# Blocks 8 to 15 of a float64 weight conversion placed in a hand-written order of steps, behind the first copies of y

## The chip, the cores and the metric

The kernel runs on one core of a Trainium2 chip. The metric is the device time of one execution in microseconds (us); lower is better. A core has five engines with an instruction stream each: PE (matmul; its weight loads are listed as PEld), DVE (vector), ACT (scalar), POOL and SP. SP, ACT and POOL also issue DMA transfers. Each engine takes its instructions in program order, and an instruction waits at the head of its stream until what it reads has been written and what it overwrites has been read.

## What is computed

Two blocks follow each other. The first filters every channel of `x` along the sequence in the frequency domain; the second is a small feed-forward network with the activation h * sigmoid(h).

```python
X = np.fft.rfft(x, axis=1)                     # x: (8, 3008, 256)
y = np.fft.irfft(X * (filt_r + 1j * filt_i)[None], n=3008, axis=1)
t = y.reshape(24064, 256)
h = t @ w_in                                   # (256, 2048)
g = h * (1.0 / (1.0 + np.exp(-h)))
return (g @ w_out).astype(np.float32)          # (2048, 256)
```

`w_in` and `w_out` reach the kernel as float64, two 32-bit words per value. The chip's engines work in float32 here, so the kernel converts them itself.

## The kernel before

**Tiles.** The 2048 hidden channels are 16 blocks of 128 (j = 0 to 15), in 8 pairs (jp = 0 to 7). The tokens of a batch are two halves of three token pairs each, 48 token pairs in all. One *step* is one token pair with one pair of blocks, so there are 384 steps, and the first eight (steps 0 to 7) are the first token pair with jp = 0 to 7. Both products use a scheme of seven multiplications in place of eight: a step has seven `hidden` matmuls (line 974), and one step later seven `project` matmuls (line 1041) that add up the output in PSUM. The scheme needs sums of weights (S1 to S4, `combine_weights`), sums of tokens (`tokens`, tile `ty`), and sums of the activated values `g` (all on DVE, line 945).

**A step** has eight rounds (0 to 7). `hidden` and `project` yield after each matmul, so that one matmul of each stands in a round. `hidden` copies the partial sums out of the bank `px` three times on ACT (lines 982, 989, 995, tile `abc`), adds them to the bank `pyz` on DVE (line 945: g0 in round 1, g2 in round 4, g1 in round 7) and applies the activation on ACT (line 978). `px` and `pyz` have one buffer each, so the next step's first matmul on `pyz` waits until DVE has read g1.

**Other work** is hung into this order by `put(step, round, piece)`: it is issued when that round is reached. Here belong the seven remaining pieces of batch 1's first transform, `stage1(u)` (line 413, tile `pa`: two matmuls of 512 columns; line 418: two copies on ACT; line 426: four stores on POOL, `store_rows`), at steps u - 1, round 3, for u = 2 to 7.

**Conversion of a weight block** (512 values in each of 128 partitions) splits each float64 into exponent and mantissa:

- `bits_of_weights`, DVE, lines 1173 and 1175: exponent bits `e` and mantissa bits `m` from the high word.
- `convert_weights`, ACT, lines 1180 and 1181: both to float. For blocks 0, 2 and 6 two more on ACT, lines 1186 and 1187.
- `round_weights`, DVE, line 1193: the low word added to the mantissa; line 1195 (other blocks): the exponent to the bits of a power of two; line 1199: the sign put on it.
- `place_weights`, DVE, line 1208: mantissa times power, two multiplications of 256 columns, into `w_t`, the weights for the matmuls.

Then `combine_weights(jp)` forms four sums of a pair of blocks, DVE, four additions of 256 columns (line 945).

**The stretch that the change touches** begins after batch 0's transforms. `stage3(g)` for g = 0 to 3 (line 715, tile `pd`) makes the first half of y; eight copies (line 729) bring it to SBUF, two of them on DVE (g = 2 and 3, h = 1), six on ACT. Before `stage3` there are idle matmuls (`idle_wide`, line 1279) that compute nothing. The order in the source is, shortened:

```python
placed(4, 5); rounded(6, 7); placed(6, 7)
rounded(8); placed(8)
gp.tensor_copy(out=gate, in_=w_t[:, 4, A11, 0, 0:1])
for u in range(2): second["store_rows"](u)
idle_wide(12)
for g in range(4): part["stage3"](g)
nc.sync.dma_start(out=wi_t, in_=wi_dram.ap())
second["load_x"](2); weights(10, 11, 12); second["load_x"](3); weights(13)
```

The copy to `gate` (POOL, line 1364) holds the stores of batch 1's first two pieces, which come behind it on POOL, until block 8 is placed. The load of `wi_t` (SP, line 1370) overwrites a table that `stage3` reads, and so holds the loads behind it on SP. Once the order of steps begins, blocks 9 to 15 are converted one per step: block j at step j - 9, its bits, float conversion and rounding in round 1, its placing in round 5.

Of the kernel before, what the change touches and what calls it, by code (L numbers as in the profile page):

```python
# [65 lines left out]
LAG = 1  # L66

A11, A12, S3, A22, S1, S2, S4 = range(7)
ROUNDS = 8


# [49 lines left out]
def laid_out(inputs):  # L121

    row = np.empty((128, 2 * NG), int)
    p = np.arange(128)
    for j in range(4):
        s0, tau = slot_residue(0, 0, j), (1 if j % 2 == 0 else -1)
        for half in range(2):
            off, t = (s0, tau) if half == 0 else (94 - s0, -tau)
            mine = p[(p // 32 == j) & (p % 2 == half)]
            row[mine] = off + t * np.arange(2 * NG) + 94 * np.arange(16)[:, None]  # L130
    filt = np.stack([inputs["filt_r"][row], inputs["filt_i"][row]], axis=1)
    w_in, w_out = inputs["moe_w_in"], inputs["moe_w_out"]
    w_in = w_in.reshape(128, 2, NJ, 128).transpose(2, 0, 1, 3).reshape(NJ, 128, 256)
    moe_w = np.concatenate([w_in, w_out.reshape(NJ, 128, 256)], axis=2)
    return dict(x=inputs["x"], x_first=first_quarters(inputs["x"][0]), filt_a=filt[:, :, 0:4], filt_b=filt[:, :, 4:], moe_w=moe_w)


# [124 lines left out]
def kernel(  # L262
# [64 lines left out]

    w_t = cpool.tile([128, NJP, 7, 2, 128], FP32)
    warm = cpool.tile([128, 1], FP32)
    bias_t = cpool.tile([128, 5], FP32)  # L330
    gate = cpool.tile([128, 1], FP32)
    x_all = xpool.tile([128, 2, 2, 2 * C], FP32)
# [23 lines left out]
    def spectral(b):  # L356
# [304 lines left out]
        def rows_first(g):  # L661

            if g in (2, 3):
                room = t4pool.tile([128, 4, C], FP32, name=f"q_{b}_{g}", tag="t4")
                tiles = room[:, 0:2], room[:, 2:4]
            else:
                tiles = [pool.tile([128, 2, C], FP32, name=f"q_{b}_{g}_{i}", tag=tag) for i, (pool, tag) in
                         enumerate(((zpool, "z"),) * 2 if g == NG - 1 else ((qpool, "q"), (opool, "o")))]
            for i, qt in enumerate(tiles):
                copy, queue = (nc.scalar.copy, nc.scalar) if i == 0 or g < 4 else (nc.vector.tensor_copy, nc.sync)  # L670
                copy(out=qt, in_=halves[g][i])
                a0 = 8 * g + 4 * i
                queue.dma_start(out=d2[a0:a0 + 4].rearrange("a n h c -> (a n) h c"), in_=qt)
# [119 lines left out]
    def put(step, rnd, piece, *args):  # L793

        pending.append((step + rnd / ROUNDS, len(pending), lambda: piece(*args)))

    last_part = [None]

    def plan(b, part):
# [2 lines left out]

        if b == 1:
            for u in range(2, 8):
                put(at + u - 49, 3, part["stage1"], u)
        else:
            put(at - {2: 80, 3: 120}.get(b, 128), 0, part["reverse_x"])
            early_fold = (-73, ((-68, 3), (-68, 5), (-67, 5), (-66, 5))), (-89, ((-82, 5), (-81, 3), (-81, 5), (-75, 5)))
# [211 lines left out]
    def project(step):  # L1020
# [16 lines left out]
        for c, k, i, h in order:  # L1037
            if i not in acc[pair]:
                acc[pair][i] = accps.tile([128, 2, 256], FP32, name=f"acc_{pair}_{i}", tag=f"a{i}")

            nc.tensor.matmul(out=acc[pair][i][:, h, 0:n], lhsT=w_t[:, jp, c, 1], rhs=g[:, k, 0:n],  # L1041
                             start=(jp == 0 and h == 0), stop=last, skip_group_check=True)
            if last and pair == len(pairs) - 1:
                drain_last(pair, i, h, n, acc[pair])
            elif last and (h == 1 or i == 3):
                drain(pair, i)
            yield
# [66 lines left out]

    PLACES = (((A11, 1), (A11, 2)), ((S3, 1), (A12, 2)))
    raws = {}

    def places(j, w):  # L1120
        first, by = PLACES[j % 2][w]
        return w_t[:, j // 2, first:first + by + 1:by, w]

    def columns(ap, w):

        if w == 0:
            return ap.rearrange("p (k n) -> p k n", k=2)
        return ap.rearrange("p (q k i) -> p k q i", q=4, k=2)

    def load_weights(j, queue=None):  # L1130

# [22 lines left out]
    def bits_of_weights(*js):  # L1154

        for j in js:
# [9 lines left out]
            else:  # L1166
# [2 lines left out]
            lo, hi = words[:, :, 0], words[:, :, 1]  # L1169
            ef, mf = e.bitcast(FP32), m.bitcast(FP32)  # L1170
            ends = (lo, hi) if j in (2, 3, 6, 7) else (m, e)
            raws[j] = lo, hi, e, m, ef, mf, ends[0].bitcast(FP32), ends[1].bitcast(FP32), ends[1]
            v.tensor_scalar(out=e, in0=hi, scalar1=20, scalar2=0x7ff,
                            op0=ALU.logical_shift_right, op1=ALU.bitwise_and)
            v.tensor_scalar(out=m, in0=hi, scalar1=0xfffff, scalar2=None, op0=ALU.bitwise_and)

    def convert_weights(*js):
        for j in js:
            _, _, e, m, ef, mf, *_ = raws[j]
            nc.scalar.activation(out=ef, in_=e, func=AFT.Relu, bias=bias_t[:, 0:1])  # L1180
            nc.scalar.activation(out=mf, in_=m, func=AFT.Identity, scale=2.0 ** -20, bias=1.0)
        for j in js:
            if j in (0, 2, 6):

                e, ef = raws[j][2], raws[j][4]
                nc.scalar.activation(out=ef, in_=ef, func=AFT.Relu, scale=-1.0, bias=bias_t[:, 1:2])
                nc.scalar.activation(out=e, in_=ef, func=AFT.Identity, scale=-float(1 << 23),
                                     bias=bias_t[:, 2:3])

    def round_weights(*js):  # L1190
        for j in js:
            lo, hi, e, m, ef, mf, mo, _, _ = raws[j]
            v.scalar_tensor_tensor(out=mo, in0=lo, scalar=2.0 ** -52, in1=mf, op0=ALU.mult, op1=ALU.add)
            if j not in (0, 2, 6):
                v.tensor_scalar(out=e, in0=ef, scalar1=255.0, scalar2=float(1 << 23),
                                op0=ALU.min, op1=ALU.mult)
        for j in js[::-1]:
            hi, e, eo = raws[j][1], raws[j][2], raws[j][8]
            v.scalar_tensor_tensor(out=eo, in0=hi, scalar=0x80000000, in1=e,
                                   op0=ALU.bitwise_and, op1=ALU.bitwise_or)  # L1200

    def place_weights(*js, eng=None):
        for j in js:
            mo, eo = raws.pop(j)[6:8]
            for w in range(2):
                cols = slice(256 * w, 256 * w + 256)
                dst = places(j, w) if w == 0 else places(j, w).rearrange("p k (q i) -> p k q i", q=4)
                (eng or v).tensor_tensor(out=dst, in0=columns(mo[:, cols], w), in1=columns(eo[:, cols], w),  # L1208
                                         op=ALU.mult)

    def load_exact(j):
        for k in range(2):
            nc.sync.dma_start(out=places(j, 0)[:, k], in_=moe_w[j][:, 128 * k:128 * k + 128])
            nc.sync.dma_start(out=places(j, 1)[:, k].rearrange("p (q i) -> p q i", q=4),
                              in_=columns(moe_w[j][:, 256:512], 1)[:, k])

    def combine_weights(jp, part=None, eng=None):

        eng = eng or v

        def w(c):
            return w_t[:, jp, c]
        if part != 1:
            combine(eng, w(S1), w(S3), w(A22), ALU.add)
            combine(eng, w(S2), w(S1), w(A11), ALU.subtract)
# [13 lines left out]
    def converted(*js):  # L1239
        if wide:  # L1240
            convert_weights(*js)

    def split(*js):
        bits(*js)
        converted(*js)

    def rounded(*js):
        if wide:
            round_weights(*js)

    def placed(*js, eng=None):
        if wide:
            place_weights(*js, eng=eng)
        else:
            for j in js:
                load_exact(j)
# [3 lines left out]
    wx3_t = qpool.tile([128, 2, C], FP32, name="wx3", tag="q").rearrange("p a c -> p (a c)")[:, 0:384].rearrange(  # L1260
        "p (k m) -> p k m", k=3)
    nc.scalar.dma_start(out=wx3_t, in_=wx3_dram.ap())
    for i, value in enumerate((-896.0, 255.0, 255.0 * (1 << 23))):
        nc.gpsimd.memset(bias_t[:, i:i + 1], value)
    for j in range(4):
        for i in range(2):
# [86 lines left out]
    weights(9)  # L1353
    for u in range(2):
        second["stage1"](u, False)
    converted(6, 7)
    converted(8)
    rounded(4, 5)
    placed(4, 5)
    rounded(6, 7)  # L1360
    placed(6, 7)
    rounded(8)
    placed(8)
    gp.tensor_copy(out=gate, in_=w_t[:, 4, A11, 0, 0:1])
    for u in range(2):
        second["store_rows"](u)
    idle_wide(12)
    for g in range(4):
        part["stage3"](g)
    nc.sync.dma_start(out=wi_t, in_=wi_dram.ap())  # L1370
    second["load_x"](2)
    weights(10, 11, 12)
    second["load_x"](3)
    weights(13)
    early[0] = None
    plan_rest(0, part)
    for g in (4, 5):
# [3 lines left out]
        put(step, 0, lambda t=t, dram=dram: nc.sync.dma_start(out=t, in_=dram.ap()))  # L1381
    for b in range(1, B):
        plan(b, second if b == 1 else spectral(b))
    for j in range(9, NJ):
        if j < 12:
            put(j - 9, 1, lambda j=j: (split(j), combine_weights(j - 8), rounded(j)))
        else:
            put(j - 9, 1, lambda j=j: (split(j), rounded(j)))
        put(j - 9, 5, placed, j)
        if j % 2:  # L1390

            put(*((j - 8, 5) if j < 15 else (j - 9, 6)), combine_weights, j // 2, 0)
            put(*{13: (j - 8, 7), 15: (j - 8, 1)}.get(j, (j - 7, 5)), combine_weights, j // 2, 1)

        if j < 11:
            put(j - 9, 1, weights, j + 5)

    per = len(PAIRS) * 2

# [76 lines left out]
```

## Time and profile before

| what | value |
|---|---|
| median of three runs | 2507.9 us (2505.73 to 2509.2) |
| the profiled execution's own time | 2507.82 us |
| span in its profile (first to last instruction) | 2506.0 us |
| PE busy | 2485.7 us (99%) |
| DVE busy | 1764.2 us (70%) |
| ACT busy | 1095.1 us (44%) |
| POOL busy | 430.8 us (17%) |
| first `hidden` matmul (step 0) | 63.93 us after the span's start |
| first `hidden` matmul of step 8 | 127.49 us |

The profile lists every instruction of one execution with its start and duration, and what ended the idle time ahead of it. A window table gives the busy time of each engine in a stretch, the granted TensorE clock (PEclk, 1.00 is full speed) and how busy the DMA engines were. The chain of waits follows the work back from the last instruction. Instructions of one engine overlap a little, so the distance from one start to the next (the *pitch*) is shorter than a duration. DMA queues are named q1 (SP), q10 (ACT), q0 (POOL) and q8 (PE's own instructions).

### The profile page before, as it was taken

The page shows a single profiled execution, that of the slowest core. Times are in us where ns is not written, and L with a number is a line of the kernel's source. Part 1 is how long each engine was busy: PE and PEld are TensorE (multiplying, and loading weights), DVE is VectorE, ACT ScalarE, POOL GpSimd, SP SyncE. Part 2 cuts the span into 40 slices and gives each one's busy share as a digit, 9 for nine tenths or more (in the row PEclk, how much of TensorE's full clock was granted, in tenths as well). Part 3 has the DMA queues.
Part 4 walks back from the last instruction along what each step waited for, and adds up shares of the span by engine and source line. Part 5 has one row for each costly group of instructions (what it writes and reads, how often), then busy time and mean ns, then how long its engine had stood idle before and what let it go on. Part 6 is the DMA issues. An engine that isn't in the chain of part 4 may idle for free.

```text
span 2506.0 us, 42228 instructions
## 1 busy us (share of the span) xinstructions
PE 2485.7 (99%) x16196; PEld 2128.4 (85%) x16196; DVE 1764.2 (70%) x3633; ACT 1095.1 (44%) x3011; POOL 430.8 (17%) x674
## 2 busy tenths in 40 slices
PE   8999999999999999999999999999999999999999
PEld 6688888888888888888888888888888888888988
DVE  8866677777767777777777867777677767655544
ACT  4444444444444444444444444444444444444443
POOL 2211212112121121211222112211121111101100
PEclk9999999999999999999999999999999999999999
DMA  8522232213232032420334203321142211200000
GB/s 304 156 67 95 73 85 64 76 51 80 61 89 77 26 88 52 115 65 15 89 67 104 58 26 82 87 68 43 27 110 58 55 43 34 64 21 9 17 9 17
DMA packets 139802, 170.68 MB, mean 68 GB/s; under 512 B 20860, under 2 KB 113372, under 8 KB 138716
## 3 DMA queue, kind: packets, MB, share of 16 engines
q1 hardware_dynamic: 115536, 120.77, 18.2%
q0 software_dynamic: 22080, 44.10, 6.8%
q8 instruction: 127, 2.08, 0.3%
q10 hardware_dynamic: 1984, 3.11, 0.3%
q14 instruction: 75, 0.61, 0.1%
HBM read 96.06 MB, written 81.26 MB: 71 GB/s over the span
## 4 chain that ended last, share of the span: by engine, by line
PE 96%; DVE 2%; ACT 1%; DMA 0%; issue 0%; POOL 0%; SPq 0%; DVEq 0%; ACTq 0%
PE acc L1041 45%; PE px L974 26%; PE pyz L974 19%; PE pd L751 1%; PE pf L483 1%; PE pc L579 1%; PE pb L541 1%; DVE g L945 1%; PE pc L657 0%; PE pa L389 0%; PE pb L523 0%; DMA w_t<-in_x_first_dram 0%; DVE w_t L1208 0%; DVE w_t L945 0%; PE pc L637 0%
## 5 line engine op out<-in xcount | busy, mean ns | idle before, releaser
L1041 PE MATMUL acc<-g,w_t 128*128 128x256 f32 (+1 forms) x5376 | 1507.8, 376 | 3.0 <-ACT o L764 2.5
L1041 PEld LDWEIGHTS acc<-g,w_t 128*128 128x128 f32 x5376 | 1016.4, 190 | 154.1 <-ACT o L764 15.3
L945 DVE TENSOR_TENSOR g<-pyz,abc 128x256 f32<-128x256 f32 (+1 forms) x1152 | 479.7, 416 | 476.9 <-ACT abc L995 236.5
L945 DVE TENSOR_TENSOR g<-g 128x256 f32<-128x256 f32 (+3 forms) x1152 | 590.6, 513 | 196.7 <-ACT g L978 183.6
L974 PE MATMUL px<-ty,w_t 128*128 128x256 f32 (+1 forms) x2304 | 677.9, 376 | 1.1 <-ACT abc L989 0.6
L978 ACT ACTIVATE g<-g 128x256 f32<-128x256 f32 (+1 forms) x1152 | 472.9, 411 | 238.1 <-DVE g L945 238.1
L945 POOL TENSOR_TENSOR s<-s 128x256 f32<-128x256 f32 (+1 forms) x329 | 252.4, 785 | 1418.9 <-DVE s L1059 1093.4
L974 PEld LDWEIGHTS px<-ty,w_t 128*128 128x128 f32 x2304 | 434.2, 190 | 59.9 <-ACT abc L989 3.9
L974 PE MATMUL pyz<-y,w_t 128*128 128x256 f32 (+1 forms) x1536 | 452.4, 376 | 1.2 <-DVE g L945 1.1
L974 PEld LDWEIGHTS pyz<-y,w_t 128*128 128x128 f32 x1536 | 283.5, 189 | 46.0 <-DVE g L945 5.8
L989 ACT COPY abc<-px 128x256 f32<-128x256 f32 (+1 forms) x384 | 141.3, 368 | 368.1 <-PE px L974 368.1
L978 ACT ACTIVATE g<-px 128x256 f32<-128x256 f32 (+1 forms) x384 | 145.8, 380 | 303.3 <-PE px L974 303.3
L995 ACT COPY abc<-px 128x256 f32<-128x256 f32 (+1 forms) x384 | 141.5, 368 | 308.5 <-PE px L974 308.4
L974 PE MATMUL px<-y,w_t 128*128 128x256 f32 (+1 forms) x768 | 227.9, 378 | 2.5 <-DVE y L729 2.5
L974 PE MATMUL pyz<-ty,w_t 128*128 128x256 f32 (+1 forms) x768 | 226.0, 376 | 0.2 <-DVE g L945 0.2
L974 PEld LDWEIGHTS px<-y,w_t 128*128 128x128 f32 x768 | 144.1, 190 | 24.3 <-issue 2.6
L974 PEld LDWEIGHTS pyz<-ty,w_t 128*128 128x128 f32 x768 | 142.2, 190 | 21.5 <-DVE g L945 1.0
L982 ACT COPY abc<-px 128x256 f32<-128x256 f32 (+1 forms) x384 | 135.1, 352 | 37.0 <-PE px L974 37.0
L503 POOL DMA_DIRECT2D d<-tf x96 | 48.5, 506 | 216.0 <-DVE tf L433 210.6
L1059 ACT COPY s<-acc 128x512 f32<-128x512 f32 (+1 forms) x94 | 54.2, 577 | 47.6 <-issue 28.5
L600 POOL DMA_DIRECT2D d<-low x36 | 22.3, 618 | 286.3 <-DVE low L596 286.3
L473 DVE TENSOR_TENSOR uf<-x_all 120x512 f32<-120x512 f32 (+1 forms) x72 | 60.2, 864 | 0.3 <-issue 0.3
(141 smaller groups left out, 1356.8 us busy)
## 6 DMA issues: line engine op xcount, KB each, us to landing
t<-d SPq DMA_DIRECT2D x84, 256.0 KB
t<-d SPq DMA_DIRECT2D x224, 96.0 KB
out_dram<-s SPq DMA_DIRECT2D x64, 256.0 KB
d<-q POOLq DMA_DIRECT2D x48, 256.0 KB, 5.3
x_all<-in_x_dram SPq DMA_DIRECT2D x96, 96.0 KB
x_all<-xr SPq DMA_DIRECT2D x96, 96.0 KB
d<-tf POOLq DMA_DIRECT2D x96, 96.0 KB, 2.7
d<-tq POOLq DMA_DIRECT2D x96, 96.0 KB, 2.8
```

The lines of the kernel that those rows point to most:

```text
L473: nc.vector.tensor_tensor(out=out, in0=in0, in1=in1, op=op)
L483: nc.tensor.matmul(out=ps[q][32 * k:32 * k + 32], lhsT=wq_t[rows, k], rhs=rhs[k][rows], start=True, stop=True)
L503: nc.gpsimd.dma_start(out=d1[par, :, grp, at:at + 4], in_=part[rows].rearrange("p q n c -> p (q n) c"))
L541: nc.tensor.matmul(out=ps[k, ri][32 * j:32 * j + 32, a, :], lhsT=dn_t[rows, 4 * (g + a) + at, :], rhs=t2s[g + a][rows, at, :], start=True, ...
L945: eng.tensor_tensor(out=out, in0=in0, in1=in1, op=op)
L974: nc.tensor.matmul(out=out, lhsT=w_t[:, jp, c, 0], rhs=rhs, start=start, stop=True, skip_group_check=True)
L978: nc.scalar.activation(out=g[:, k, 0:n], in_=g[:, k, 0:n] if src is None else src, func=AFT.Silu)
L982: nc.scalar.copy(out=sums[:, 0, 0:n], in_=xo)
L989: nc.scalar.copy(out=sums[:, 1, 0:n], in_=xo)
L995: nc.scalar.copy(out=sums[:, 2, 0:n], in_=xo)
L1041: nc.tensor.matmul(out=acc[pair][i][:, h, 0:n], lhsT=w_t[:, jp, c, 1], rhs=g[:, k, 0:n], start=(jp == 0 and h == 0), stop=last, skip_group ...
L1059: copy(out=s[:, 2 * i:2 * i + 2, 0:n], in_=acc[pair][i][:, :, 0:n])
```

## The change

- **Layout.** `laid_out` on the host reorders the weights, so that `place_weights` is a single operation of 512 contiguous columns per block. In `w_t` the output halves of A12 and S3 change places (`OUT_PLACE`).
- **Integer mantissas.** The mantissa stays an integer with its leading one put in by line 1175's second operation; the factor 2^-20 goes into the placing. ACT no longer converts mantissas. Both exponent operations are on ACT for every block, and line 1195 is gone.
- **Order.** Behind the placing of block 7 come the copies of y on DVE and the token sums at once. Block 8 (its bits and exponent are still done ahead), and blocks 9 to 15, are spread over steps 0 to 6 in a written list, in smaller pieces.
- **One copy moves** from DVE to ACT (`rows_first`, g = 4, second half).
- **Loads.** `load_x(2)`, block 10, `load_x(3)`, blocks 11 and 12 are issued directly behind block 9's load, ahead of the load of `wi_t`. Block 13 follows at step 1, 14 and 15 at step 2.
- **Batch 1's pieces** u = 2 to 7 stand one step earlier, at steps u - 2.
- **Gate and idle matmuls.** `gate` reads block 7's weights. 15 idle matmuls instead of 12 ahead of `stage3`, and 2 new ones behind it.

```diff
-                put(at + u - 49, 3, part["stage1"], u)
+                put(at + u - 50, 3, part["stage1"], u)
...
-            v.tensor_scalar(out=m, in0=hi, scalar1=0xfffff, scalar2=None, op0=ALU.bitwise_and)
+            v.tensor_scalar(out=m, in0=hi, scalar1=0xfffff, scalar2=0x100000, op0=ALU.bitwise_and,
+                            op1=ALU.bitwise_or)
     def convert_weights(*js):
         for j in js:
...
+            nc.scalar.activation(out=ef, in_=e, func=AFT.Relu, scale=-1.0, bias=bias_t[:, 0:1])
+            nc.scalar.activation(out=e, in_=ef, func=AFT.Relu, scale=-float(1 << 23), bias=bias_t[:, 1:2])
+    def add_weights(*js):
+        for j in js:
+            lo, m, mo = raws[j][0], raws[j][3], raws[j][5]
+            v.scalar_tensor_tensor(out=mo, in0=lo, scalar=2.0 ** -32, in1=m, op0=ALU.mult, op1=ALU.add)
...
+            v.scalar_tensor_tensor(out=places(j), in0=mo, scalar=2.0 ** -20, in1=eo, op0=ALU.mult, op1=ALU.mult)
...
+    second["load_x"](2)
+    weights(10)
+    second["load_x"](3)
+    weights(11, 12)
     converted(6, 7)
     converted(8)
     rounded(4, 5)
     placed(4, 5)
     rounded(6, 7)
     placed(6, 7)
-    rounded(8)
-    placed(8)
-    gp.tensor_copy(out=gate, in_=w_t[:, 4, A11, 0, 0:1])
+    gp.tensor_copy(out=gate, in_=w_t[:, 3, S3, 0, 0:1])
     for u in range(2):
         second["store_rows"](u)
-    idle_wide(12)
+    idle_wide(15)
     for g in range(4):
         part["stage3"](g)
+    idle_wide(2)
     nc.sync.dma_start(out=wi_t, in_=wi_dram.ap())
-    second["load_x"](2)
-    weights(10, 11, 12)
-    second["load_x"](3)
-    weights(13)
...
-    for j in range(9, NJ):
...
+    for step, rnd, *todo in (
+            (0, 1, (combine_weights, 1)), (0, 5, (bits, 9), (added, 9)),
+            (1, 0, (converted, 9)), (1, 1, (added, 8), (signed, 8), (placed, 8), (signed, 9), (bits, 10)),
+            (1, 2, (weights, 13)), (1, 5, (combine_weights, 2), (converted, 10)),
+            (2, 1, (placed, 9), (added, 10), (signed, 10), (placed, 10), (bits, 11)),
+            (2, 2, (weights, 14, 15)), (2, 5, (combine_weights, 3), (converted, 11)),
+            (3, 1, (combine_weights, 4), (added, 11), (signed, 11), (bits, 12)),
+            (3, 5, (placed, 11), (converted, 12)),
+            (4, 1, (combine_weights, 5), (added, 12), (signed, 12), (placed, 12)),
+            (4, 5, (bits, 13), (added, 13)), (5, 0, (converted, 13)),
+            (5, 1, (bits, 14), (added, 14), (signed, 13), (placed, 13)),
+            (5, 5, (combine_weights, 6), (converted, 14)), (5, 7, (bits, 15)), (6, 0, (converted, 15)),
+            (6, 1, (signed, 14), (placed, 14), (added, 15), (signed, 15), (placed, 15)),
+            (6, 5, (combine_weights, 7))):
+        for piece, *args in todo:
+            put(step, rnd, piece, *args)
```

More of the change, by code (lines that the diff above doesn't have):

```diff
@@ L68 @@
 A11, A12, S3, A22, S1, S2, S4 = range(7)
+OUT_PLACE = {A12: S3, S3: A12}
 ROUNDS = 8
@@ L133, in laid_out @@
     w_in = w_in.reshape(128, 2, NJ, 128).transpose(2, 0, 1, 3).reshape(NJ, 128, 256)
-    moe_w = np.concatenate([w_in, w_out.reshape(NJ, 128, 256)], axis=2)
+    w_out = w_out.reshape(NJ, 128, 4, 2, 32).transpose(0, 1, 3, 2, 4).reshape(NJ, 128, 256)
+    moe_w = np.stack([w_in.reshape(NJ, 128, 2, 128), w_out.reshape(NJ, 128, 2, 128)], axis=3).reshape(NJ, 128, 512)
     return dict(x=inputs["x"], x_first=first_quarters(inputs["x"][0]), filt_a=filt[:, :, 0:4], filt_b=filt[:, :, 4:], moe_w=moe_w)
@@ L329 @@
     warm = cpool.tile([128, 1], FP32)
+    flat_w = w_t.rearrange("p j c w n -> p j (c w) n")
     bias_t = cpool.tile([128, 5], FP32)
@@ L669, in rows_first @@
             for i, qt in enumerate(tiles):
-                copy, queue = (nc.scalar.copy, nc.scalar) if i == 0 or g < 4 else (nc.vector.tensor_copy, nc.sync)
+                copy, queue = (nc.scalar.copy, nc.scalar) if i == 0 or g < 4 else (nc.scalar.copy if g == 4 else nc.vector.tensor_copy, nc.sync)
                 copy(out=qt, in_=halves[g][i])
@@ L1039, in project @@
                 acc[pair][i] = accps.tile([128, 2, 256], FP32, name=f"acc_{pair}_{i}", tag=f"a{i}")
-            nc.tensor.matmul(out=acc[pair][i][:, h, 0:n], lhsT=w_t[:, jp, c, 1], rhs=g[:, k, 0:n],
+            nc.tensor.matmul(out=acc[pair][i][:, h, 0:n], lhsT=w_t[:, jp, OUT_PLACE.get(c, c), 1], rhs=g[:, k, 0:n],
                              start=(jp == 0 and h == 0), stop=last, skip_group_check=True)
@@ L1113, with places @@
     nc.scalar.activation(out=warm, in_=warm, func=AFT.Silu)
-    PLACES = (((A11, 1), (A11, 2)), ((S3, 1), (A12, 2)))
     raws = {}
[L1120 to L1128, printed above, removed]
+    def places(j):
+        at = 4 * (j % 2)
+        return flat_w[:, j // 2, at:at + 4].rearrange("p s n -> p (s n)")
     def load_weights(j, queue=None):
@@ L1171, in bits_of_weights @@
             ends = (lo, hi) if j in (2, 3, 6, 7) else (m, e)
-            raws[j] = lo, hi, e, m, ef, mf, ends[0].bitcast(FP32), ends[1].bitcast(FP32), ends[1]
+            raws[j] = lo, hi, e, m, ef, ends[0].bitcast(FP32), ends[1].bitcast(FP32), ends[1]
             v.tensor_scalar(out=e, in0=hi, scalar1=20, scalar2=0x7ff,
                             op0=ALU.logical_shift_right, op1=ALU.bitwise_and)
-            v.tensor_scalar(out=m, in0=hi, scalar1=0xfffff, scalar2=None, op0=ALU.bitwise_and)
+            v.tensor_scalar(out=m, in0=hi, scalar1=0xfffff, scalar2=0x100000, op0=ALU.bitwise_and,
+                            op1=ALU.bitwise_or)
@@ L1177, in convert_weights @@
     def convert_weights(*js):
         for j in js:
-            _, _, e, m, ef, mf, *_ = raws[j]
-            nc.scalar.activation(out=ef, in_=e, func=AFT.Relu, bias=bias_t[:, 0:1])
-            nc.scalar.activation(out=mf, in_=m, func=AFT.Identity, scale=2.0 ** -20, bias=1.0)
+            e, ef = raws[j][2], raws[j][4]
+            nc.scalar.activation(out=ef, in_=e, func=AFT.Relu, scale=-1.0, bias=bias_t[:, 0:1])
+            nc.scalar.activation(out=e, in_=ef, func=AFT.Relu, scale=-float(1 << 23), bias=bias_t[:, 1:2])
@@ L1182, in convert_weights @@
+    def add_weights(*js):
         for j in js:
[L1183 to L1188, printed above, removed]
+            lo, m, mo = raws[j][0], raws[j][3], raws[j][5]
+            v.scalar_tensor_tensor(out=mo, in0=lo, scalar=2.0 ** -32, in1=m, op0=ALU.mult, op1=ALU.add)
@@ L1190, in round_weights @@
     def round_weights(*js):
         for j in js:
[L1192 to L1198, printed above, removed]
+            hi, e, eo = raws[j][1], raws[j][2], raws[j][7]
@@ L1199, in round_weights, with place_weights @@
             v.scalar_tensor_tensor(out=eo, in0=hi, scalar=0x80000000, in1=e,
                                    op0=ALU.bitwise_and, op1=ALU.bitwise_or)
-    def place_weights(*js, eng=None):
+    def place_weights(*js):
         for j in js:
[L1204 to L1209, printed above, removed]
+            mo, eo = raws.pop(j)[5:7]
+            v.scalar_tensor_tensor(out=places(j), in0=mo, scalar=2.0 ** -20, in1=eo, op0=ALU.mult, op1=ALU.mult)
@@ L1211, in load_exact @@
     def load_exact(j):
[L1212 to L1215, printed above, removed]
+        nc.sync.dma_start(out=places(j), in_=moe_w[j])
     def combine_weights(jp, part=None, eng=None):
@@ L1221, in w @@
         def w(c):
-            return w_t[:, jp, c]
+            first, by = {A12: (2, 3), S3: (4, -1)}.get(c, (2 * c, 1))
+            return flat_w[:, jp, first:first + 2 * by:by]
         if part != 1:
@@ L1248, in rounded, with placed @@
         if wide:
+            add_weights(*js)
             round_weights(*js)
-    def placed(*js, eng=None):
+    def placed(*js):
         if wide:
-            place_weights(*js, eng=eng)
+            place_weights(*js)
         else:
@@ L1262 @@
     nc.scalar.dma_start(out=wx3_t, in_=wx3_dram.ap())
-    for i, value in enumerate((-896.0, 255.0, 255.0 * (1 << 23))):
+    for i, value in enumerate((1151.0, 255.0 * (1 << 23))):
         nc.gpsimd.memset(bias_t[:, i:i + 1], value)
@@ L1383, with added, signed @@
         plan(b, second if b == 1 else spectral(b))
-    for j in range(9, NJ):
[L1385 to L1396, printed above, removed]
+    def added(*js):
+        if wide:
+            add_weights(*js)
+    def signed(*js):
+        if wide:
+            round_weights(*js)
+    for step, rnd, *todo in (
[14 more added lines that the diff above has]
+            put(step, rnd, piece, *args)
     per = len(PAIRS) * 2
```

## The prediction, as it was put on record

> **What bounds the kernel now.** Page first. Its top line says where the time can be:
>
> ```profile
> PE 2485.7 (99%) x16196; PEld 2128.4 (85%) x16196; DVE 1764.2 (70%) x3633; ACT 1095.1 (44%) x3011; POOL 430.8 (17%) x674
> ```
>
> PE does the same work before and after, but for five idle matmuls, so only PE's idle time (16.2 us by the gaps of its rows, nearly all before 71 us) and time at a low clock can be won. Next the chain of waits from 0 to 140 us, to see who sets the end of the conversion stretch:
>
> ```profile
> 57.65 1.31 DVE raw L1199 x2
> 58.98 1.43 DVE w_t L1208 x4
> 60.41 0.60 DVE m L1193
> 61.38 0.70 DVE e L1199
> 62.11 0.76 DVE w_t L1208 x2
> 62.87 0.93 DVE y L729 x2
> 63.93 1.19 PE px L974 x2
> ```
>
> From 46.50 to 63.8 the chain is DVE's: blocks 4 to 8 one after another, then the two copies of y, then step 0. Third PE's timeline there:
>
> ```profile
> 56.05 2.73 PE L715 MATMUL pd<-wi_t,w_t 64*64 64x47 f32 x167 [0.81 <-DMA w_t<-d]
> 59.88 1.53 PE L715 MATMUL pd<-wi_t,w_t 64*64 64x47 f32 x87 [1.10 <-issue]
> 63.93 1.19 PE L974 MATMUL px<-y,w_t 128*128 128x256 f32 x2 [2.52 <-DVE y L729]
> ```
>
> `pd` is done at 61.41 and PE then waits 2.52 for y. Inside `pd` PE stands still for 1.10 and waits for nothing that is named. The DMA view of 57.2 to 58.6 has one packet: PE's instructions (q8), from 57.29 to 58.51. Fourth the windows (PE, PEld, DVE, ACT, POOL, clock, DMA share, GB/s):
>
> ```profile
> 54.00:56.00 2.00, 0.84 (x5) 0.34 (x3) 1.97 (x7) 1.97 (x4) 0.00 (x0) 1.00 0.93 249
> 56.00:58.00 2.00, 1.95 (x129) 1.98 (x133) 1.97 (x5) 0.84 (x3) 0.00 (x0) 1.00 0.25 94
> 58.00:60.00 2.00, 0.90 (x60) 0.78 (x54) 1.97 (x6) 0.94 (x3) 0.00 (x0) 1.00 0.00 0
> 62.00:64.00 2.00, 0.07 (x1) 0.10 (x1) 1.86 (x6) 0.00 (x0) 1.04 (x3) 0.77 0.49 106
> 64.00:66.00 2.00, 2.00 (x5) 1.49 (x6) 1.43 (x3) 0.37 (x1) 2.00 (x5) 0.50 1.03 315
> 72.00:74.00 2.00, 2.00 (x8) 1.64 (x8) 1.12 (x2) 0.82 (x3) 0.00 (x0) 0.67 0.91 369
> ```
>
> Two things: the clock is at half from 63.1 (0.77 of 62 to 64) to 73.3 (0.67 of 72 to 74), and the DMA engines are idle from 57 to 62, because SP's loads are queued behind that of `wi_t`.
>
> **The change, part by part.** All times go to one mark, the first `hidden` matmul of step 8 (127.49 before); behind it both kernels do the same on PE.
>
> *DVE up to y.* The rows give these distances from start to start: 0.34 for L1173, L1175, L1195 and for 256 columns of L1208, 0.61 for L1193 and L1199. A block costs 2 x 0.34 + 0.61 + 0.34 + 0.61 + 0.67 = 2.9 now. Afterwards L1195 is gone and the placing is one operation of 512 columns, which the trace does not have. It does L1193's kind of work (two tensors and a number): 0.61, against 0.67 for the pair; with ends 0.34 and 0.67 a block moves by at most 0.27, and four blocks by 1.1, which is covered, as follows. A block is 2.5. ACT does two operations as now (1.24); if it takes both Relu at 0.62 instead of 0.62 and 0.52, still less than DVE's 2.5. From 46.50: sums of pair 0 to 48.1, bits of 6 to 8 to 50.1, blocks 4 to 7 with all their parts to 58.6. Block 8's 2.4 stand behind y now. So DVE is ready 2.8 us before `pd` ends (61.41), and is off the path. What is late next is `pd`: the last copy of y follows its last matmul by 0.6, the first `hidden` copy by 0.15, so step 0 starts at 62.2 in place of 63.93 (-1.7). The first part, up to 46.5, has the same waits (loads, POOL's z, the transposes); the copy that goes to ACT takes 0.58 at 45.3, where ACT is idle between 44.7 and 45.8: free, at worst 0.3. Fifteen idle matmuls in place of twelve fill PE to 55.8, before the data of 56.05: free. The two behind `pd` take 0.86 at full clock, 61.4 to 62.3, in time that PE waits.
>
> *Steps 0 to 7.* A matmul costs 0.43 here and a step has 14 (6.04), step 0 seven (3.0); a `pa` pair is 1.73, so steps with `pa` have a floor of 7.77. Steps now: 8.05 8.43 8.12 8.11 7.97 7.85 8.65 6.38. I laid the operations of DVE, ACT and PE behind each other in the new order at these distances, each behind what it reads and what it overwrites. For the order of before this gives 127.8 for step 8 (0.3 too long), and 125.7 if the clock had been full: the low clock costs 1.8 to 2.1. The new order at full clock gives 6.0, 8.2, 8.0, 8.0, 7.8, 8.0, 7.7 and 6.7, in sum 60.5. What is over the floor is the next step's `pyz` waiting for DVE to read g1, because four sums (1.46) or the bits and the added low word stand between g2 and g1; step 6 has 7.9 of DVE work. ACT converts exponents alone, so the wait of 0.97 for ACT's mantissa (101.39, L1193) goes in every step. Sum so far: 62.2 + 60.5 = 122.7, against 127.8 by the same working: -5.1.
>
> *Stores, one step earlier `pa`.* `pa` u = 2 in step 0 writes the tiles of u = 0, which POOL's stores must have left. They are issued behind `gate`, now at 58.6 (63.19 before, landing 7.4 later). Up to 65.5 they cost nothing, and each us behind that one us. Issued 4.5 us earlier, they should land at 65 to 66: I take 0, at most 2.
>
> *Loads ahead of* `wi_t`. Two pieces of x (0.39 MB each) and blocks 10, 11, 12 (0.52 MB each), 2.36 MB, were issued from 61.85 on. Now SP issues them directly behind block 9's load (52.30), so they are in the queue when the DMA engines run empty at 56.4: at the 315 GB/s of window 64 to 66 that is 7.5 us of full load, across PE's instruction fetch. What does the fetch cost in a full queue? The instruction that starts at 59.88 is the first of a block; 256 records (matmuls and weight loads) earlier PE was at 56.6, and the packet came at 57.29, 0.7 later. Counted back in 256s, earlier blocks are entered at 18.9, 28.1, 35.1 and 42.5, and their packets came at 20.62, 31.06, 39.32 and 43.79: 1.7, 3.0 and 4.2 later with the DMA share over 1.0, and 1.3 at 0.63. (There PE needed the block only later.) So the added wait *a* is bounded by 0 (the fetch comes ahead) and 6.8 (all of the backlog), with rows at 1.0, 2.3 and 3.5. I take 1.0, from the row of 20.62: there too the queue held SP's loads of x and raw blocks alone, and stayed full behind the fetch, while the 39.32 row stood among stores of another queue too. Step 0 then starts at 63.2 and step 8 at 123.7.
>
> In that case PE stands still for 2.1 in `pd`, and the clock may fall: before, it fell at 63.1 behind gaps of 1.10 and 2.52. If it falls, the two idle matmuls take 1.7 and step 0 starts at 64.0; half speed for a while costs 0.8 to 1.3 in all, since DVE sets part of these steps. I take the middle between falling and not, mean 124.5.
>
> The Trainium skill (DMA: Bandwidth & Descriptors, Queues, rings and completion order) says that a DMA engine goes round its queues by whole packets, typically 9 to 17 descriptors each. By that the fetch would wait for one turn, not for the backlog; with 4 KB descriptors on 16 engines, an estimate from that page, a turn is 0.6 to 1.1 MB, 1.9 to 3.5 us at the row's 315 GB/s, and step 8 would come at 126.0 to 127.8. The rows of 1.7 to 4.2 agree in size. The Trainium skill (Runtime: NRT & Kernel Launch, Instruction fetch mechanics) calls the cost of a block's end mostly hidden; the 1.10 of this trace, in matmuls so short that 256 records last 2.2 us, speaks against it here, and by that page the sum would stay at 122.7.
>
> **Sum.** 124.5 - 127.8 = -3.3; the profiled execution's own time is 2507.82 (its span 2506.0 and 1.82 outside), so **2504.5**. The median of the runs, 2507.9, is the same within 0.1.
>
> **Rivals.** 0.2%, 5.0 us, is about what a measurement of this kernel can tell from no change; faster ends at 2502.9, slower begins at 2512.9.
>
> - *The fetch comes ahead of the loads* (a below 0.5). For: 16 KB against loads of 400 KB; against: three rows. 122.7 to 123.2: 2502.7 to 2503.2.
> - *The fetch waits longer*, a 1.7 to 3.5, as at 31.06 and 39.32, and the clock falls for one or two windows of some 3.4 us. 125.6 to 127.7: 2505.6 to 2507.8. For: also POOL's stores of before, issued from 63.19 behind the same loads, show one packet up to 67.5.
> - *Slower: the fetch waits for the whole backlog.* Place: PE in `pd`. Price: 7.5 us behind 2.36 MB, a = 6.8, step 8 at 131.1 with the low clock: 2511.1. It decides from a = 3.5, where the gain is used up. For: the 39.32 packet came when the queue had all but drained. Against: the packets of 20.62 and 31.06 came while it was full.
> - *The steps run at PE's floor.* For: my working is 0.3 too long for before. Steps 1 to 5 at 7.77 would be 59.3 in sum: 121.4 without a (2501.4), 122.4 with a = 1.0 (2502.4).
> - *It does not do what it says*: y is free of block 8 but `pd` ends the stretch. This is already in the sum, 1.7 in place of 2.5.
>
> **How the numbers follow.** Forecast 0.36, fetch ahead 0.25, longer fetch 0.18, floor 0.14, whole backlog 0.07. Faster by over 0.2%: the floor and 0.15 of the fetch ahead, 0.29. Slower by over 0.2% needs a near 6.8 and late stores: 0.05. Same: 0.66. The range reaches from the floor at 2501.5 to the longer fetch with stores 0.7 late, 2508.5; beyond lie the backlog and half of the floor.
>
> **What would show it.** Right: DVE done with block 7 by 59, L729 released by PE; a gap of some 2 us inside `pd` with q8's packet near 58.3; step 0 at 63 to 64, steps of 7.7 to 8.2, step 8 near 124.5. Wrong: a gap of 1.1 (fetch ahead) or 3 and more; `t` on ACT (L418) in step 0 released by a DMA (late stores); steps 1 to 5 at 7.8 (floor); DVE later than PE at y (the placing dearer than 0.61); and other times behind step 8, where I cost everything at nothing.

## The result, and the profile after

The changed kernel takes 2512.3 us (median; 2510.47 to 2513.12), the kernel before 2507.5 in the same comparison: a ratio of 1.0018, 95% interval 1.0010 to 1.0027. It is slower by 4.8 us, where 3.3 faster was forecast, and outside the range (2501.5 to 2508.5). The profiled execution has a span of 2510.7. The first line of its page shows that PE's work is the same but for the five idle matmuls (ten records of each kind), and DVE's is 8 us less:

```profile
PE 2488.4 (99%) x16206; PEld 2133.9 (85%) x16206; DVE 1756.2 (70%) x3603; ACT 1095.5 (44%) x3006; POOL 431.0 (17%) x673
```

The chain of waits of the kernel after, over the stretch that was shown of before (start, length, what):

```profile
52.76 3.84 DMA w_t<-d
56.74 2.63 PE pd L718 x161
59.36 5.48 issue
64.85 2.81 PE pd L718 x92
67.65 2.00 PE idle L1267 x4
69.66 0.85 PE px L977 x2
```

DVE has left this stretch of the chain, as the change means it to. In its place stands one piece without a named cause, "issue", 5.48 long, in the middle of `pd` (it was 1.10). The windows of the kernel after (PE, PEld, DVE, ACT, POOL, clock, DMA share, GB/s) show what went on meanwhile:

```profile
56.00:58.00 2.00, 1.41 (x87) 1.31 (x87) 2.00 (x5) 1.04 (x3) 0.00 (x0) 1.00 0.94 301
58.00:60.00 2.00, 1.36 (x92) 1.24 (x84) 0.47 (x1) 1.63 (x4) 1.41 (x3) 1.00 0.99 268
60.00:62.00 2.00, 0.00 (x0) 0.00 (x0) 0.00 (x0) 0.00 (x0) 2.00 (x5) 1.00 1.15 256
62.00:64.00 2.00, 0.00 (x0) 0.00 (x0) 0.00 (x0) 0.00 (x0) 1.00 (x3) 0.77 0.95 268
64.00:66.00 2.00, 1.15 (x44) 1.15 (x48) 0.00 (x0) 0.02 (x1) 0.00 (x0) 0.50 0.97 340
72.00:74.00 2.00, 2.00 (x5) 1.31 (x5) 1.32 (x4) 0.69 (x2) 0.00 (x0) 0.67 0.00 0
```

From 60 to 64 PE, DVE and ACT do nothing at all, while the DMA engines, idle in this place before, are full. DVE stops in the window from 58 on (0.47 busy): blocks 4 to 7 are ready by 58.5, as forecast. The DMA view of 57.2 to 61.9 in this trace shows what filled the engines:

```profile
q1 hardware_dynamic: 339, 1.23, 103.1%
```

Only SP's queue moved: no packet of q8 (PE's instructions) and none of POOL's stores, six of which were issued in that time. The q8 packet came at 61.99, and PE went on at 64.85. The clock is at half from 63.1 to 73.3, as long as before, but now it also slows `pd` and the idle matmuls.

The account to the start of step 8 (127.49 before, 131.47 after), from PE's timelines:

| piece | before | after | difference |
|---|---|---|---|
| `pd` starts behind its first two matmuls | 56.05 | 56.74 | +0.69 |
| `pd` up to the gap | 2.73 | 2.63 | -0.10 |
| gap in `pd` | 1.10 | 5.48 | +4.38 |
| rest of `pd` | 1.53 | 2.80 | +1.27 |
| end of `pd` to step 0 | 2.52 | 1.80 | -0.72 |
| steps 0 to 7 | 63.56 | 62.02 | -1.54 |
| sum | | | +3.98 |

Behind step 8 there is 0.7 more, in two single steps (129 and 185). Three of the experiments' profiles (runs 2, 3 and 7) do not have it; run 3 is one with the changed steps and the earlier `pa`, so I count it as scatter.

### The profile page after: what moved, and what is told of

The parts are those of the page before. It is cut to its first block, busy times and chain, and to the rows that moved or that the text cites. A ratio compares the mean times of both kernels' runs of the same rounds, so it can differ in the third digit from the quotient of the medians.

```text
span 2510.7 us, 42210 instructions
## 1 busy us (share of the span) xinstructions
PE 2488.4 (99%) x16206; PEld 2133.9 (85%) x16206; DVE 1756.2 (70%) x3603; ACT 1095.5 (44%) x3006; POOL 431.0 (17%) x673
## 4 chain that ended last, share of the span: by engine, by line
PE 97%; DVE 1%; DMA 1%; issue 0%; ACT 0%; SPq 0%; POOL 0%; DVEq 0%; ACTq 0%
PE acc L1044 45%; PE px L977 26%; PE pyz L977 19%; PE pd L754 1%; PE pf L486 1%; PE pc L582 1%; PE pb L544 1%; PE pa L392 0%; PE pa L416 0%; DMA w_t<-in_x_first_dram 0%; PE pd L718 0%; DMA w_t<-d 0%; DVE g L948 0%; PE pb L526 0%; PE pc L640 0%
```

## Experiments

PE's own instructions come in packets of 16384 bytes on q8: each profile has 127 of them, one for each border between blocks of 256 PE records. The theory after the result: PE's next instruction block is asked for when PE enters the block before it, and this request waits in the DMA engines behind the loads that SP issued; the five loads ahead of `wi_t` are the cause. Rivals: POOL's stores, now issued inside `pd`; a border of the instruction block moved by the three more idle matmuls; and, for what is left over, the other parts of the change.

**1. All five loads back** behind the load of `wi_t`.

```diff
-    second["load_x"](2)
-    weights(10)
-    second["load_x"](3)
-    weights(11, 12)
...
     nc.sync.dma_start(out=wi_t, in_=wi_dram.ap())
+    second["load_x"](2)
+    weights(10)
+    second["load_x"](3)
+    weights(11, 12)
```

> The changed kernel with one thing undone: the loads of two x pieces and blocks 10, 11, 12 are again issued behind the load of wi_t, so behind pd. Theory (PE's instruction block waits behind SP's queued loads): the DMA engines run empty near 56.5, the q8 packet comes 0.7 to 1.1 us after pd enters the block before, the gap inside pd falls from 5.48 to 1.0 to 1.5, step 0 starts at 62.2 to 62.9, step 8 at 122.7 to 123.4, the clock stays full, and the time is 4 to 5 us below the kernel before (about 2503). Rival (POOL's stores, now issued from 58.77 inside pd, hold the fetch): they stand where they stood, the gap stays above 4 and the time near 2512. Rival (three more idle matmuls moved the block's border to a worse place): the gap stays near 5.5, the time near 2512.

Measured: 2509.2, ratio 1.0006 (0.9997 to 1.0015). PE's timeline of this run:

```profile
57.32 2.63 PE L718 MATMUL pd<-wi_t,w_t 64*64 64x47 f32 x161 [0.83 <-DMA w_t<-d]
61.48 1.65 PE L718 MATMUL pd<-wi_t,w_t 64*64 64x47 f32 x93 [1.53 <-issue]
64.02 0.60 PE L977 MATMUL px<-y,w_t 128*128 128x256 f32 x2
68.16 3.37 PE L416 MATMUL pa<-x_all,wx_t 96*128 96x512 f32 x4 [1.61 <-DMA x_all<-in_x_dram]
```

The gap in `pd` fell from 5.48 to 1.53, with stores and block border where they were: both rivals fall for the gap. But the time came down by only 3, not by some 9. The last line tells why in part: `pa` stands one step earlier now and reads x in step 0, and x is late. PE waits 1.61, the clock falls for 3.4 us, and step 0 takes 9.89. I had not thought of that: two parts of the change need each other. The eleven executions reach from 2506.1 to 2511.7, and the time goes with the granted clock: its mean over the execution is 1.000 in the three shortest and 0.998 in the five longest. So the median mixes executions with and without a long fall of the clock, and the profile shows one of them, of 2509.2.

**2. The early loads alone**, in the kernel before (the same five loads behind block 9's, ahead of `wi_t`).

> The kernel before with one part of the change alone: two x pieces and blocks 10, 11, 12 are loaded directly behind block 9, ahead of wi_t. Theory (queued loads): the gap inside pd grows from 1.10 to about 5, pd ends near 65.5 in place of 61.41, so that pd and not DVE ends the stretch; step 0 at about 66 in place of 63.93, the low clock some us longer, and the time 2 to 4 us above the kernel before (2509.5 to 2511.5). Both rivals (stores, block border): neither gate nor idle matmuls are touched, so the gap stays 1.1 and the time 2507.5.

Measured: 2512.2, ratio 1.0020 (1.0011 to 1.0029), and a gap of 6.16:

```profile
58.68 2.73 PE L715 MATMUL pd<-wi_t,w_t 64*64 64x47 f32 x167 [0.63 <-DMA w_t<-d]
67.56 2.59 PE L715 MATMUL pd<-wi_t,w_t 64*64 64x47 f32 x87 [6.16 <-issue]
```

The early loads alone cost 4.9 us, where 2 to 4 were expected. In the profiled execution, at 2515.0 the longest of the eleven, the clock fell for 13.7 us behind the gap, and for another 3.4 at 13.0, ahead of all that was changed.

**3. A smaller dose**: only the two pieces of x ahead of `wi_t`, blocks 10, 11, 12 behind it.

> The changed kernel with a smaller dose: only the two x pieces (0.79 MB) are loaded ahead of wi_t, blocks 10, 11, 12 behind it. Theory in the form that the fetch waits for what was issued before it: of block 9 and x some 0.36 MB are left when the fetch is asked for near 57.2, 1.3 us at 280 GB/s, so the packet comes near 58.5, the gap is 1.8 to 2.5 and the time 2504 to 2506. Theory in the form that any full queue costs a fixed turn of some 4 us: gap 4 to 5.5 and 2510 to 2512. Rivals (stores, block border): gap and time as in the changed kernel, 5.5 and 2512.

Measured: 2508.8, ratio 1.0007 (0.9999 to 1.0016), gap 3.48:

```profile
62.56 2.71 PE L718 MATMUL pd<-wi_t,w_t 64*64 64x47 f32 x93 [3.48 <-issue]
```

Neither form of the theory had this number; the table below takes it up.

**4. The gate behind y**: `gate` copied from y, so that the stores are issued only after `pd` (the first at 68.85, `pd` ends at 68.16).

> The changed kernel with its early loads, but POOL's gate reads the last columns of y, so that the eight stores are issued only behind pd. One look for the gap. Theory (queued loads): the gap inside pd stays at 5 to 5.5 and the q8 packet near 62. Rival (stores): the gap falls to 1 to 2 and the packet comes near 58. Either way the stores land later, pa's copies of step 0 wait for them, and the time may be 2 to 5 us above the changed kernel's or below it by the gap.

Measured (one run, 2511.2): gap 6.13, packet at 62.53.

```profile
65.36 2.80 PE L718 MATMUL pd<-wi_t,w_t 64*64 64x47 f32 x93 [6.13 <-issue]
```

Without any store in the queues the fetch is as late. The stores are not the cause.

**5. Only the piece of x that step 0 reads** ahead of `wi_t`.

> The changed kernel, in which only the one piece of x that step 0's pa reads is loaded ahead of wi_t; block 10, the other piece and blocks 11 and 12 stand behind it. Theory (the fetch waits for what SP issued before it, and pa one step earlier needs its x early): some 0.3 MB stand ahead of the fetch, so it waits 1.5 to 2 us and the gap is 2 to 2.6; pa of step 0 does not wait for x (1.61 with all loads back); step 0 at 63.5 to 64.5 and 6 to 7.5 long, step 8 at 124.5 to 126, time 2504.5 to 2507. Rival (a fixed turn as soon as anything is queued): gap as with both pieces of x, 3.5, and 2508 to 2509.

Measured: 2506.7, ratio 0.9998 (0.9989 to 1.0007). In the profiled execution (2505.8) the gap is 1.65, less than the 2 to 2.6 expected; there is no wait for x, the clock is full throughout the stretch, step 0 is 6.37 long and step 8 comes at 124.78:

```profile
61.56 1.65 PE L718 MATMUL pd<-wi_t,w_t 64*64 64x47 f32 x93 [1.65 <-issue]
```

The dose counts, not the mere presence of a load. Here too the executions scatter, from 2504.6 to 2511.6, with a mean clock of 1.000 in the three shortest and 0.998 in the two longest.

**6. Loads back, and pa back** to steps u - 1. The loads are moved as in run 1; the other part of the edit is:

```diff
-                put(at + u - 50, 3, part["stage1"], u)
+                put(at + u - 49, 3, part["stage1"], u)
```

> The changed kernel with two parts undone: the five loads behind wi_t, and batch 1's pieces of pa at steps u - 1 again. Theory: with late loads only the earlier pa was left without its x (step 0 took 9.89); so here the gap in pd is 1.1 to 1.6, nothing waits for x, step 0 starts at 62.3 to 64 and takes 6 or less at full clock, step 8 comes at 122.7 to 124.5, and the time is 3 to 4.5 us below the kernel before (2503 to 2504.5): the new order of DVE's work alone gains. Rival (the new order of blocks 8 to 15 itself costs, and not the loads): step 8 not before 126 and the time within 1 of the kernel before.

Measured: 2502.6, ratio 0.9980 (0.9971 to 0.9988): faster than the kernel before by 5.0 and than the changed one by 9.7, and a little more than expected. PE's timeline of this run:

```profile
56.49 2.63 PE L718 MATMUL pd<-wi_t,w_t 64*64 64x47 f32 x161 [0.43 <-DMA w_t<-d]
60.03 1.64 PE L718 MATMUL pd<-wi_t,w_t 64*64 64x47 f32 x93 [0.91 <-issue]
61.61 1.13 PE L1267 MATMUL idle<-d_t,wx_t 96*128 96x256 f32 x4
62.57 0.60 PE L977 MATMUL px<-y,w_t 128*128 128x256 f32 x2
```

And two of its windows, with the columns as above:

```profile
58.00:60.00 2.00, 1.12 (x76) 1.00 (x68) 0.47 (x1) 1.39 (x4) 1.41 (x3) 1.00 0.00 0
72.00:74.00 2.00, 2.00 (x9) 1.42 (x8) 1.95 (x5) 1.73 (x4) 0.31 (x1) 1.00 0.87 221
```

The DMA engines are idle again from 58 to 60, the fetch waits 0.7, the clock stays at 1.00, and step 8 comes at 121.49. The new order of DVE's work and its shorter arithmetic gain what they were to gain; the loss sits in the loads and in `pa`. How much of the gain is the order's and how much the arithmetic's no run separates, and some 2 us of it, by the prediction's own working (1.8 to 2.1), come from the clock, which no longer falls.

**7. As 6, and the copy of pc on DVE again.**

> As the run with loads and pa undone, and also the one copy of pc (g = 4, second half) on DVE again in place of ACT. Theory: with the copy on ACT, the store of the next copy (ACT's queue) is issued 1.1 later than before (47.73 against 46.62) and pd's last data come at 56.5 to 57.3 in place of 56.05; here pd's second wait ends near 56.1, and step 8 and the time are 0.4 to 1.2 lower than with the copy on ACT. Rival (pd's later start is scatter of the loads ahead of it): pd's start as there, no difference in time.

Measured: 2502.4, ratio 0.9978 (0.9969 to 0.9987): no difference from 6. From the first `pb` behind its wait to the third matmul of `pd` it is 31.2 us here, 30.1 before, 30.8 after, and 30.3 to 31.4 in runs 1, 3, 5 and 6 with the copy on ACT. My theory of the late store falls; the 0.69 in the account is scatter of the data that `pd` waits for.

**8. The block border moved**: 20 narrow idle matmuls, 80 records, at the start of the changed kernel.

```diff
     idle(18)
+    narrow = bank(0, "idle").rearrange("p a c -> p (a c)")
+    for _ in range(20):
+        nc.tensor.matmul(out=narrow[:, 0:8], lhsT=wx_t, rhs=wx_t[:, 0:8], start=True, stop=True)
```

> The changed kernel with 20 narrow idle matmuls (8 columns each, 80 records of matmuls and weight loads) added at the very start of PE's work, where PE waits for loads: this moves the borders of PE's instruction blocks by 80 records. One look. Theory (the gap stands at the border of an instruction block whose fetch waits in the queue): the stall comes after some 123 of pd's matmuls, not 163; its fetch is asked for before pd starts, so it waits behind less and the gap is shorter (1 to 4); a second gap stands near the last of pd's 256 matmuls, or ahead of the idle matmuls behind them. Rival (the gap belongs to something in pd, its data or its banks): it stays behind the 163rd matmul, at 5 to 6 us.

PE's timeline of this run:

```profile
62.53 4.04 PE L718 MATMUL pd<-wi_t,w_t 64*64 64x47 f32 x251
71.71 0.46 PE L718 MATMUL pd<-wi_t,w_t 64*64 64x47 f32 x5 [5.14 <-issue]
```

The gap left its place behind the 163rd matmul and stands behind the 251st, at the next border, and is longer than the 1 to 4 expected; at the 123rd, where the first border now falls, there is none, as that block was fetched at 58.16, before the loads were issued. So the stall belongs to the instruction block, not to what `pd` computes. (The narrow matmuls took 6.2 us and the start slipped, so the time, 2516.3, is no measure here.)

**9. Only pa back**, the loads early.

> The changed kernel with only batch 1's pieces of pa at steps u - 1 again; the loads stay early. With the runs that undid loads alone and both, this fills the square of the two parts. Theory (the early loads cost some 4 us at the fetch, the earlier pa 1.8 us by itself, as step 0 grows from 4.6 to 6.4 and step 6 gives back only 0.4): gap 5 to 6, clock at half for one to three windows of 3.4 us, steps 58.9 in sum plus 1 to 2 for the clock, time 1 to 2.5 us below the changed kernel's 2512.3, so 2510 to 2511.5. Rival (the earlier pa costs only because its x came late when the loads were undone): no gain from this, 2512 to 2513.

Measured: 2510.3, ratio 1.0011 (1.0003 to 1.0020), gap 5.95. The square of the two parts, with the new order in all four:

| | `pa` at u - 2 | `pa` at u - 1 |
|---|---|---|
| loads ahead of `wi_t` | 2512.3 (changed kernel) | 2510.3 (run 9) |
| loads behind `wi_t` | 2509.2 (run 1) | 2502.6 (run 6) |

The early loads cost 7.7 us with `pa` where it was; the earlier `pa` costs 2.0 with its x in time and 6.6 with its x late, by the medians. As run 1 scatters with its clock, the last figure is a mixture: by the shortest execution of each it is 4.2 (2506.14 against 2501.93).

**10. As 6, with 12 idle matmuls and none behind `pd`.**

> The run with loads and pa undone, and besides 12 idle matmuls ahead of pd in place of 15 and none behind it. The prediction cost the idle matmuls at nothing. Theory: they end before pd's data (55.9 against 56.5) and lie in the wait for y, so time and step 8 agree with that run within 0.5, unless the clock falls without them: PE then idles 0.8 to 1.0 more ahead of pd and 0.9 behind it, as it did in the kernel before, where the clock fell for 10.2 us and cost about 2. With the fall: 1 to 2.5 us slower than 2502.6. The border of the instruction block also moves back by 6 and 14 records, which should change the gap by less than 0.2.

Measured: 2502.5, ratio 0.9979 (0.9970 to 0.9988), step 8 at 121.51, the clock full. The five idle matmuls are worth nothing here, and gaps of 1.29, 1.24 and 0.78 do not bring the clock down.

**What the fetch waits for.** In every profile the stalled instruction is PE's record 1473 (1729 in run 8), counted from 0 over matmuls, weight loads and the 23 records of PE's own sequencer, so the request can be dated to the record 256 earlier. The date may be late: elsewhere packets come up to 37 records ahead of what it gives (0.6 us taken from request to packet), and in `pd` 37 records last 0.3 us, an estimate. The loads counted are those of SP from block 9's on; "wait" goes from the request to the packet, and the last column of bytes has what moved from the packet's start until PE went on:

| run | loads issued by the request, MB | moved during the wait, MB | moved from the packet until PE goes on, MB | wait, us | gap, us |
|---|---|---|---|---|---|
| before | 0.52 | 0.02 | 0.00 | 0.67 | 1.10 |
| 6 | 0.52 | 0.10 | 0.00 | 0.69 | 0.91 |
| 5 | 0.92 | 0.20 | 0.03 | 1.32 | 1.65 |
| 3 | 1.31 | 0.66 | 0.02 | 3.25 | 3.48 |
| after | 2.88 | 1.25 | 0.72 | 4.77 | 5.48 |
| 9 | 2.88 | 1.25 | 0.63 | 5.43 | 5.95 |
| 4 | 2.88 | 1.34 | 0.69 | 5.45 | 6.13 |
| 2 | 2.88 | 1.40 | 0.77 | 5.48 | 6.16 |
| 8 | 2.88 | 1.24 | 0.66 | 4.69 | 5.14 |

With little queued the fetch waits for all of it (runs 5 and 3). With much queued it waits until 1.24 to 1.40 MB have moved, and comes ahead of the rest. Order of issue does not explain the rest: in run 8 the last load was issued 1.8 us ahead of the request and 0.66 MB still came behind the packet. A turn of a certain length per queue fits all rows of the table; its length was not varied by itself, so that it is a turn is argued, not shown.

The Trainium skill (DMA: Bandwidth & Descriptors, Queues, rings and completion order) states such a turn: a DMA engine drains a whole packet of one queue, typically 9 to 17 descriptors and at most 64, before it goes to the next. 1.24 to 1.40 MB are 303 to 342 rows of 4 KB, over 16 engines 19 to 21 descriptors each, an estimate: by kind the traces agree, by size they lie above the typical figure and within the ceiling.

## Why the prediction was wrong, step by step

- **The fetch (a = 1.0): the step that failed.** The mechanism was named and its rows were laid out, 1.0, 2.3 and 3.5 more; then I took the smallest, "from the row of 20.62", because its queue held SP's loads alone. The added wait was 4.1 (4.77 against 0.67), above all three rows. The row nearest to it was that of 39.32 (3.5), by which the forecast would have read "no gain". The reason given for the row of 20.62 does not single it out: at 31.06, too, only SP's queue moved, and 0.75 MB followed in the 2 us behind the packet. The DMA view of before shows both, from the record to the packet (18.92 to 20.62, then 28.1 to 31.06):

```profile
q1 hardware_dynamic: 235, 0.70, 105.6%
q1 hardware_dynamic: 345, 1.21, 102.6%
```

Counted in bytes, the larger rows tell what `pd` then showed: 1.21 MB at 31.06, 1.27 at 39.32 (on two queues), 1.25 in `pd`. What differs is the rate, 409 and 302 GB/s there and 262 in `pd`; 1.21 MB at 262 GB/s would have been 4.6 us. The prediction carried over the microseconds, and at that the shortest. Why the fetch at 20.62 had to let only 0.70 MB pass, with 0.81 MB behind it, stays open.

- **The clock.** Half a clock "for a while" was put at 0.8 to 1.3. After a gap of 5.48 it fell for 10.2 us. Against run 5, which has the same instructions at full clock, that is 1.2 on the rest of `pd` (2.80 and 1.64), 0.9 from there to step 0 (1.80 and 0.90) and 1.35 on the steps (62.02 and 60.67). Together some 3.4: the term was about a third of what it is, and it depends on the first one, the gap. The sum has a small slip here, too: with 0.8 to 1.3 in all, the middle between falling and not is 124.1 to 124.4; 124.5 comes out only if the 0.8 of the idle matmuls is added besides.
- **From 124.5 to 131.47.** Of these 7.0 us some 3.4 are the gap (5.48 where 2.1 was forecast), 2.6 the clock, 0.7 the later data of `pd` and 0.2 the steps.
- **The rival on the slow side** had the right place and sign and, at 2511.1, nearly the time, but by luck: its wait of 6.8 was 4.1, its clock of some 1.6 was 3.4. Its mechanism, waiting for the whole backlog, is wrong (0.6 to 0.8 MB came behind the packet), and its point of decision, a = 3.5, too high: run 3, with a at 2.6, is already no faster than before. It had 0.07 where the trace's own rows deserved far more.
- **DVE up to y: right.** The placing in one operation takes 0.60 from start to start (0.61 forecast), `gate` is released by block 7 at 58.53 (58.6 forecast), and `pd` ends the stretch.
- **The copy to ACT and the idle matmuls: right** to cost them at nothing (runs 7 and 10).
- **The steps: right in sum, wrong in what was not asked.** Forecast at full clock 6.0, 8.2, 8.0, 8.0, 7.8, 8.0, 7.7, 6.7; run 5 has 6.37, 8.19, 8.03, 8.03, 7.87, 7.93, 7.71, 6.54. But the sum was never made for `pa` left in its place: run 6 has 4.60 in step 0 and 8.07 in step 6, and 58.92 in all, 1.75 less than run 5. The earlier `pa` adds 1.77 to step 0, takes 0.36 from step 6, which DVE sets, and step 7 is 0.35 longer (6.54 against 6.19); in the sum this loss lay hidden under the gain of the rest.
- **Loads and pa together** were costed apart. The x that step 0's `pa` reads must come early, the loads must not stand ahead of the fetch: only run 5's single piece meets both, and it gains nothing for it.
- **Late stores: right** at 0. In the changed kernel they landed from 66.19 on, and ACT's copies of `pa` in step 0 (74.21 and 75.07) waited for PE. In run 5, where step 0 starts at 64.10, the four that matter had landed by 63.12, and the copies (67.53 and 68.39) waited for PE as well.
- **Fetch unhindered, 2502.7**, was the value of the new order with everything else free. Run 6 gives 2502.6, with `pa` put back. That the two agree within 0.1 is luck: in its profile the steps are 1.6 shorter than the 60.5 of the sum, step 0 starts 0.4 later, and 0.8 more than before lies behind step 8.
- **PE's idle time.** Of the 16.2 us, 11.8 lie ahead of 71 us, not nearly all; no term of the sum rests on it.

## What to carry to other kernels

A load that is moved ahead can cost more than its own data path: a transfer that is asked for while the load is queued may have to wait for it, and an engine's own instructions are such a transfer (4.8 us here). Where a stretch has many short instructions (here 256 records in 2.2 us), look for a gap that ends on "issue", count records to find the block border, and leave the DMA engines idle across it. Carry a wait in a queue from one place to another in bytes and the rate there, not in microseconds. When several parts of a change are costed, make the sum once more without each part: the one that loses hides under those that gain.

## What the runs showed of the hardware that was not expected

- A queue with some 2 MB left held a 16 KB fetch for 4.7 to 5.5 us, until 1.24 to 1.40 MB had passed, and let it in ahead of the rest.
- PE went on 1.3 to 1.6 us behind the end of the q8 packet (1.37 before, 1.52 after, 1.27 in run 3), so even with little or nothing queued a fetch inside `pd` cost 0.9 to 1.5 (runs 6 and 1). The Trainium skill (Runtime: NRT & Kernel Launch, Instruction fetch mechanics) calls the cost of a block's end mostly hidden; in each of the twelve profiles one border inside `pd` showed as a gap.
- The clock fell for 3.4, 6.8 or 10.2 us at a time after gaps of 3.48 and more, after two gaps of 1.53 and 1.61 (run 1), and after 1.10 and 2.52 (before); it stayed full with 1.16 and 1.65 (run 5) and with 1.29, 1.24 and 0.78 (run 10). These are single profiled executions, and the mean clocks of runs 1 and 5 show that executions of one kernel differ in this, so the list gives no limit.
